# Fifteen small loads behind a copy on ScalarE, in a gated mix of cached attention and a mixer MLP

## The chip, the cores and the metric

The kernel runs on one core of one Trainium2 chip. The metric is the device time of one execution in microseconds (us). The trace is that of one profiled execution; its times count from the start of its span.

## The reference

The inputs are a token `x` for each of two batches (1024 wide), a key and a value cache of 32768 positions (4 key/value heads, 32 query heads, head width 128), and the weights of an attention block A and of a mixer block B. All is fp32. Cut to what matters:

```python
g = sigmoid((x * gate_w).sum(-1))
q = (x @ wq)                                   # 32 heads of 128
a = softmax(q k^T / sqrt(128)) v @ wo          # 8 query heads share a key head
h2 = gelu(layernorm(x1) @ w3) @ w4             # the mixer's MLP
out = g * a + (1 - g) * (x1 + h2)
```

With one position for each batch the mixer's shifts leave zeros, so `x1` is `x`, and `w1` and `w2` are not needed. The caches are by far the most bytes: 8 pairs of batch and head, each with 16 MB of keys and 16 MB of values.

## The kernel before

**The ring.** SBUF holds two large buffers, `load0` and `load1`, 64 KB on each of 128 partitions. All that is read passes through them in halves, two rows of 32 KB side by side for each partition: `wq` (2 halves), `w3` (2), then for each of the 8 pairs the keys `kt` (2 halves) and the values `vt` (2), with `w4` between the fourth and the fifth pair, and `wo` at the end (its last part into a buffer `tail`). A half of a cache or of `wq` is one load of 8 MB; a half of `w3` has 7 MB.

**Who issues.** SyncE (SP) issues all of these loads, in a fixed order, on its own queue, which the profile calls q1. Each load waits on a semaphore that says that its buffer has been read: the half of `kt` for pair 0 waits for TensorE's projection with the `w3` half that lay there; the half of `vt` waits for the scores made from the `kt` half. So at most two loads are in flight or waiting to be read. Two other transfers exist: ScalarE's load of `xg` (the token and the gate's weights, 128 rows of 96 bytes) at the start, on ScalarE's queue, which the profile calls q10, and the store of the output at the end (8 rows of 1 KB), on q1.

**The prologue.** TensorE multiplies `x` by the two halves of `wq` (function `project`, L361, into `sc0` and `sc1`). VectorE copies `sc0` and ScalarE `sc1` to SBUF (L402 and L404, `d_q` and `a_q`). VectorE reorders them (L410), TensorE transposes them (L416), VectorE spreads them into `q_pad` (L424). Then TensorE multiplies the normalised `x` by the halves of `w3`, VectorE copies `sc2` and ScalarE `sc3` (L438 and L440, `d_h` and `a_h`), VectorE reorders (L445, it waits for both), TensorE transposes (L453), VectorE and ScalarE make the gelu (L457 to L472; the Tanh, L462, on ScalarE).

**The turns.** For each pair, `turn` (L479) multiplies the queries by the two halves of `kt` (L488), finds the maximum, lets ScalarE make the exponentials (L555), transposes them (L505), and multiplies them by the two halves of `vt` (L514). On TensorE turn 0 stands behind the prologue's last transposes in program order.

**Waiting.** Each engine runs its instructions in order. `Line.after` puts a wait in front of the engine's next instruction, once for each semaphore value; `Line.mark` raises the engine's own semaphore by one. A load raises its semaphore by 16 when it has landed entirely.

Of the kernel before, what the change touches and what calls it, by code (L numbers as in the profile page):

```python
# [73 lines left out]
def kernel(  # L74
# [52 lines left out]
    nc = tc.nc  # L127
    scale = DH ** -0.5

    def new(name, *shape, parts=P):  # L130
        return nc.alloc_sbuf_tensor(name, [parts, *shape], F32).ap()

    def bank(name):
        return nc.alloc_psum_tensor(name, [P, 512], F32).ap()
# [45 lines left out]
    f = new("f", REP)  # L180
    so_far = new("so_far", D // G)
    out_sb = new("out_sb", 2, CHUNK)

    sc = [bank(f"sc{i}") for i in range(NI)]
    tr = [bank(f"tr{i}") for i in range(2)]
# [9 lines left out]
    def sem(name):  # L195
        cleared.append(nc.alloc_semaphore(name))
        return cleared[-1]

    stored = nc.alloc_semaphore("stored")
    pe, dve, act, pool = (Line(e, sem(n)) for e, n in (  # L200
        (nc.tensor, "pe"), (nc.vector, "dve"), (nc.scalar, "act"), (nc.gpsimd, "pool")))
# [2 lines left out]
    landed = [sem(f"landed{i}") for i in range(2)]  # L204
    w_in = [*landed, sem("w_in2")]
    got_x = sem("got_x")
    issued = sem("issued")
    copied = sem("copied")
    middle = slice(BASE, BASE + 2 * ROWS)
# [192 lines left out]
    d_q = dve.mark(nc.vector.tensor_copy(row[:, 0], sc[0]))  # L402
    act.after(done)
    a_q = act.mark(nc.scalar.copy(row[:, 1], sc[1]))  # L404

    twice = p.rearrange("p i t w q -> p (i t w q)")[:, :REP * P * 2].rearrange(
        "p (h w i q) -> p h w i q", h=REP, w=PART, i=2)
# [33 lines left out]
    n = KF // G  # L441
# [234 lines left out]
```

## Time and profile before

| what | value |
|---|---|
| time, median of 2 runs | 773.13 us (773.12 to 773.14) |
| profiled execution, its own time | 773.23 us |
| its span in the trace | 771.7 us |
| TensorE busy | 437.3 us (57%) |
| VectorE busy | 94.1 us (12%) |
| ScalarE busy | 60.6 us (8%) |
| bytes read | 331.36 MB, mean 429 GB/s over the span |

The profile's page gives the busy time of each engine, the span in 40 slices with the share of time in which the 16 DMA engines were busy, and the DMA queues. The timeline lists instructions as start, duration, engine, line, operation, and in brackets how long the engine had been idle and what ended it. An answer on a window lists the DMA packets that began in it for each queue: number, MB, and their time as a share of 16 engines over the window.

### The profile page before, as it was taken

What the parts mean: (1) busy time and instruction counts of PE and PEld (TensorE: products, weight loads), DVE (VectorE), ACT (ScalarE), POOL (GpSimd) and SP (SyncE); (2) the same over time, 40 slices, a digit from 0 to 9 for tenths busy, and PEclk for the clock granted to TensorE, in tenths of its full rate; (3) what the DMA queues carried; (4) which work ended last, traced back from release to release, by engine and by line L of the source; (5) the groups of instructions that cost most, each with busy time, mean ns of one, the idle gap of its engine ahead of it and who ended that gap; (6) DMA issues with size and microseconds to landing.
All of it is one profiled execution on the core that took longest, in us unless ns stands there. A gap on an engine that the chain in (4) does not pass through costs nothing. (4 is left out here: it accounts for less than half of the span.)

```text
span 771.7 us, 7439 instructions
## 1 busy us (share of the span) xinstructions
PE 437.3 (57%) x3332; PEld 201.3 (26%) x3332; DVE 94.1 (12%) x269; ACT 60.6 (8%) x144; POOL 3.9 (1%) x13
## 2 busy tenths in 40 slices
PE   0576756564645474556575446454745565646467
PEld 0232413231322232223233213121322222313134
DVE  1110202100210021002100002100210021002110
ACT  0000002000200020002000002000200020002000
POOL 2000000000000000000000000000000000000000
PEclk9977668767787768767766678777777687678788
DMA  9999999999999999999999999999999999999997
GB/s 381 435 436 436 435 436 435 432 436 431 435 431 431 435 435 431 435 435 435 427 431 440 432 435 435 435 435 435 435 435 435 435 435 435 435 428 435 425 428 323
DMA packets 6648, 331.50 MB, mean 430 GB/s; under 512 B 872, under 2 KB 1008, under 8 KB 1264
## 3 DMA queue, kind: packets, MB, share of 16 engines
q1 hardware_dynamic: 6496, 331.36, 99.4%
q8 instruction: 7, 0.11, 0.1%
q10 hardware_dynamic: 144, 0.01, 0.0%
q14 instruction: 1, 0.01, 0.0%
HBM read 331.36 MB, written 0.01 MB: 429 GB/s over the span
## 5 line engine op out<-in xcount | busy, mean ns | idle before, releaser
L488 PE MATMUL sc<-load,q_cur 128*32 128x512 f32 x1024 | 145.7, 728 | 131.0 <-PEq L53 131.0
L514 PE MATMUL pv<-load,pt 128*32 128x512 f32 x1024 | 134.4, 684 | 89.4 <-PEq L53 89.4
L488 PEld LDWEIGHTS sc<-load,q_cur 128*32 128x32 f32 x1024 | 52.5, 131 | 218.0 <-issue 212.7
L514 PEld LDWEIGHTS pv<-load,pt 128*32 128x32 f32 x1024 | 40.0, 124 | 173.7 <-issue 173.7
L505 PE MATMUL sc<-wide,p 128*128 128x128 f32 x256 | 43.8, 344 | 22.8 <-PEq L53 22.8
L571 DVE TENSOR_REDUCE mx<-sc 128x1 f32<-128x512 f32 x32 | 21.4, 689 | 285.0 <-PE sc L488 285.0
L555 ACT ACT_TABLE_LOAD x8 | 10.3, 1283 | 484.0 <-ACTq L53 484.0
L505 PEld LDWEIGHTS sc<-wide,p 128*128 128x128 f32 x256 | 39.6, 182 | 30.0 <-issue 30.0
L371 PE MATMUL acc<-load,w_pad 128*32 128x256 f32 x448 | 34.5, 481 | 18.6 <-PEq L53 18.6
L588 DVE COPY pt<-sc 64x256 f32<-64x256 f32 x64 | 25.9, 414 | 80.3 <-PE sc L505 79.7
L561 ACT COPY pt<-sc 64x256 f32<-64x256 f32 x64 | 23.5, 367 | 84.3 <-PE sc L505 81.8
L593 DVE COPY pv_sb<-pv 128x512 f32<-128x512 f32 x16 | 10.3, 686 | 146.8 <-PE tr L520 146.8
L371 PEld LDWEIGHTS acc<-load,w_pad 128*32 128x32 f32 x448 | 18.9, 138 | 33.4 <-issue 28.5
L524 PE MATMUL tr<-sel,pv_sb 128*128 128x8 f32 x128 | 18.7, 282 | 11.8 <-PEq L53 11.8
L357 PE MATMUL sc<-load,x_pad 128*32 128x512 f32 x128 | 18.9, 756 | 6.8 <-PEq L53 6.8
L555 ACT ACTIVATE p<-sc,bias 128x512 f32<-128x512 f32 x32 | 21.5, 685 | 0.1
L524 PEld LDWEIGHTS tr<-sel,pv_sb 128*128 128x128 f32 x128 | 18.2, 226 | 12.3 <-issue 12.3
L357 PE MATMUL sc<-load,xn_pad 128*32 128x384 f32 (+1 forms) x128 | 15.7, 651 | 7.7 <-PEq L53 7.7
L342 PE MATMUL tr<-xg_sb,perm 128*128 128x16 f32 x4 | 1.0, 372 | 23.0 <-DMA xg_sb<-xg 23.0
L584 DVE COPY p<-p 128x256 f32<-128x256 f32 x32 | 9.4, 294 | 26.7 <-ACT p L555 26.7
L357 PEld LDWEIGHTS sc<-load,x_pad 128*32 128x32 f32 x128 | 4.9, 135 | 20.0 <-issue 20.0
L357 PEld LDWEIGHTS sc<-load,xn_pad 128*32 128x32 f32 x128 | 4.8, 131 | 18.5 <-issue 18.5
(89 smaller groups left out, 94.8 us busy)
## 6 DMA issues: line engine op xcount, KB each, us to landing
load<-w SPq DMA_DIRECT2D x4, 7168.0 KB, 24.9
load<-wo SPq DMA_DIRECT2D x1, 7168.0 KB, 29.0
load<-wo SPq DMA_DIRECT2D x1, 4608.0 KB, 19.2
load<-wo SPq DMA_DIRECT2D x1, 2560.0 KB, 24.9
tail<-wo SPq DMA_DIRECT2D x1, 1024.0 KB, 26.9
tail<-wo SPq DMA_DIRECT2D x1, 640.0 KB, 28.0
load<-kt SPq DMA_DIRECT2D x16, 29.8
load<-vt SPq DMA_DIRECT2D x16, 29.4
```

Source lines behind the costliest of these rows:

```text
L357: last = nc.tensor.matmul(b[C * g:C * g + C, :hi - lo], pad[:, k], t[:, o + lo:o + hi], start=(k == 0), stop=(k == KD - 1))
L371: inst = nc.tensor.matmul(acc[C * g:C * g + C], lhsT, rows[:, g * (D // G):(g + 1) * (D // G)], start=False, stop=last, skip_group_check=True)
L488: last = nc.tensor.matmul(sc[i][C * g:C * g + C], q_cur[:, w, s], ring[j][:, w, o:o + 512], start=(s == 0 and w == 0), stop=(s == 1 and w ...
L505: last = nc.tensor.transpose(sc[k][:, t * P:(t + 1) * P], pair.rearrange("p w q -> p (w q)"), ident)
L514: last = nc.tensor.matmul(pv[C * g:C * g + C], pt[j][w][:, lo:lo + C], ring[j][:, w, o:o + G * DH], start=(j == 0 and w == 0 and t == 0), ...
L524: last = nc.tensor.matmul(tr[1][:, w * REP:(w + 1) * REP], pv_sb[:, s, w].rearrange("p i q -> p (i q)"), sel[:, s], start=(s == 0), stop=( ...
L555: nc.scalar.activation(p[:, i, :, :PART], sc[i].rearrange("p (t q w) -> p t w q", t=NT, w=PART), AF.Exp, bias=bias, scale=scale, accum_out ...
L561: nc.scalar.copy(*halves(1, j, c)).then_inc(pt_in, 1)
L571: last = [nc.vector.reduce_max(out=mx[:, k:k + 1], in_=sc[k], axis=AX.X) for k in ((1, 2) if i == 2 else (i,))][-1]
L584: nc.vector.tensor_copy(p[:, i, :, PART], p[:, i, :, 0]).then_inc(to_pe, 1)
L588: nc.vector.tensor_copy(*halves(0, j, c)).then_inc(pt_in, 1)
L593: last = nc.vector.tensor_copy(pv_sb[:, :, :, i], pv.rearrange("p (s q w) -> p s w q", q=HALF, w=PART))
```

## The change

Behind its copy `a_q` of the product with `wq`, ScalarE waits for that copy and issues fifteen loads. Load n (1 to 15) takes the first 16 + n numbers of the first n rows of the keys of pair 0, half 0, from DRAM into a buffer of its own, `told_sb`, on n partitions. Nothing reads that buffer. All fifteen raise a new semaphore, `told`, and ScalarE waits until it stands at 15 x 16, so until all have landed, before its next instruction, the copy `a_h`. Nothing else is changed.

```diff
@@ buffers
     out_sb = new("out_sb", 2, CHUNK)
+    told_sb = new("told_sb", 15, 32, parts=16)
@@ semaphores
     got_x = sem("got_x")
+    told = sem("told")
@@ the prologue
     act.after(done)
     a_q = act.mark(nc.scalar.copy(row[:, 1], sc[1]))
+    act.after(a_q)
+    for n in range(1, 16):
+        nc.scalar.dma_start(told_sb[:n, n - 1, :16 + n], kt[0, 0, :n, :16 + n]).then_inc(told, 16)
+    act.after((told, 15 * 16))
 
```

## The prediction

> **What bounds the kernel now.** I read the page first (the span, the row of DMA shares in 40 slices, the queues), then the timeline of the first 136 us, then the DMA answers for short windows, down to nanoseconds. From the page:
>
> ```profile
> span 771.7 us, 7439 instructions
> ...
> DMA  9999999999999999999999999999999999999997
> ...
> DMA packets 6648, 331.50 MB, mean 430 GB/s; under 512 B 872, under 2 KB 1008, under 8 KB 1264
> ...
> q1 hardware_dynamic: 6496, 331.36, 99.4%
> ...
> q10 hardware_dynamic: 144, 0.01, 0.0%
> ```
>
> The reader is to see a kernel that is one stream of loads: q1 (SP's loads) keeps the 16 DMA engines busy in every slice. q10 is ScalarE's queue; its 144 packets are the one load of `xg`. An instruction anywhere costs time only if it lets q1 run dry or slows its packets; every microsecond in which q1 is dry is a microsecond of the total, since no later slice has room to win it back.
>
> The timeline around the place of the change, as start, duration, engine, line:
>
> ```profile
> 0.73 0.39 ACTq L245 DMA_DIRECT2D xg_sb<-xg  x1
> 0.73 0.88 SPq L246 DMA_DIRECT2D load<-wq  x2
> ...
> 51.97 0.58 ACT L404 COPY pt<-sc 128x512 f32<-128x512 f32 x1 [23.81 <-PE sc L357]
> ...
> 69.76 16.32 SPq L219 DMA_DIRECT2D load<-kt  x2
> ...
> 85.76 0.48 ACT L440 COPY pt<-sc 128x384 f32<-128x384 f32 x1 [33.21 <-PE sc L357]
> ...
> 86.49 2.08 DVE L445 COPY p<-pt 128x896 f32<-128x896 f32 x2
> ...
> 88.62 6.14 PE L453 MATMUL tr<-wide,p 128*128 128x8 f32 x28 [2.92 <-DVE p L445]
> ...
> 96.70 9.76 PE L488 MATMUL sc<-load,q_cur 128*32 128x512 f32 x64 [1.93 <-PEq L53]
> ...
> 106.52 18.60 SPq L219 DMA_DIRECT2D load<-vt  x2
> ...
> 116.05 8.63 PE L488 MATMUL sc<-load,q_cur 128*32 128x512 f32 x64 [9.59 <-PEq L53]
> ...
> 135.40 8.77 PE L514 MATMUL pv<-load,pt 128*32 128x512 f32 x64 [2.03 <-PEq L53]
> ```
>
> SP may load the first half of `vt` at 106.52 only because TensorE has ended the first half of turn 0 (96.70 + 9.76 = 106.46). The halves of `kt` before it have landed by 96.70 and 116.05, where TensorE stood waiting for them: 19.35 us for a load. So the issue at 106.52 comes 9.5 us before q1 would be empty. That is the slack of the stage in which the new wait lies, and it hangs on ScalarE: the copy at 85.76 (L440), VectorE's copies, TensorE's transposes, then turn 0.
>
> **How q10 is served beside q1.** The only load on ScalarE's queue tells it. Below: its landing, the two queues in the first 21.7 us, and four successive records at 21.756, 21.764, 21.772 and 21.776 us.
>
> ```profile
> xg_sb<-xg ACTq DMA_DIRECT2D x1, 12.0 KB, 22.1
> ...
> q1 hardware_dynamic: 128, 8.39, 92.3%
> q10 hardware_dynamic: 112, 0.01, 0.4%
> ...
> q10 hardware_dynamic: 1, 0.00, 18.8%
> ...
> q1 hardware_dynamic: 1, 0.00, 14.1%
> ...
> q10 hardware_dynamic: 1, 0.00, 14.1%
> ...
> q1 hardware_dynamic: 1, 0.07, 3778.1%
> ```
>
> 12 KB took 22.1 us to land. `xg` has 128 rows and 144 packets: 128 of data and 16 that raise the semaphore, 8 + 1 on each engine. By 21.7 us each engine had begun 128/16 = 8 packets of q1 and 112/16 = 7 of q10: one for one. The four records are one engine's: data of q10, semaphore of q1, semaphore of q10, the next 64 KB of q1. So an engine takes one packet from each queue in turn, semaphore packets too; a small packet itself takes some 10 ns (18.8% of 16 engines over 4 ns is 12 ns), but its turn comes only when a q1 packet is through, 19.35/8 = 2.4 us.
>
> The Trainium skill has a rule that speaks against any cost here. Its page "DMA: Bandwidth & Descriptors", section "Queues, rings and completion order", says that an engine drains a whole packet, typically 9 to 17 descriptors, from one queue before it switches. The nine of `xg` would then have gone in one turn, and the trace shows nine turns; by that rule 30 of them would be through in two to four turns (an estimate: some 10 us after the issue), and the sum below would be zero.
>
> **The change, part by part.** Removed or moved: nothing.
>
> *The issues.* ScalarE issues 15 loads from 52.6 (51.97 + 0.58). At 0.39 us each, the row of `xg`, that is 5.9 us, to 58.5; SP's rows bound one by 0.88/2 = 0.44. ScalarE idled 33.21 us there, so this is free under the present order. The bytes: 12.6 KB, nothing against 331 MB.
>
> *How many packets the busiest engine gets.* The nearest row is the store of 8 rows at the end, the one transfer with fewer than 16 rows (window from 771 us):
>
> ```profile
> DMA packets 16, 0.01 MB, mean 12 GB/s; under 512 B 8, under 2 KB 16, under 8 KB 16
> ```
>
> 8 packets of 1 KB and 8 small ones: one engine for each row, each with a semaphore packet. So loads of 1 to 15 rows make 120 + 120 packets. No row says which engines. Spread evenly, an engine gets 15 (perhaps 16); if every load begins at the same engine, that one takes part in all 15 and gets 30. I take 30: nothing in the store or the 46 other transfers shows a memory from one to the next. The low end, 15, is a rival below.
>
> The skill's page named above, section "Why a DMA increments its semaphore by 16 and not by 1", says that SP's and ScalarE's transfers use the lowest-numbered engines, as many as the largest divisor that fits. The 8 + 8 packets agree on the number; which engines, no run here shows yet. By it the figure is 30.
>
> *When the thirtieth is through.* The first is in the ring at about 53.7: q1's first 15 packets begin in the window 1.7 to 2.4 for an issue at 0.73, so 1.0 us behind the start of the issue. From there q1's packets, as begun in 53.7 to 113.5, in 113.5 to 114.0, and in 115.0 to 115.5:
>
> ```profile
> q1 hardware_dynamic: 15, 0.98, 420.3%
> ...
> q1 hardware_dynamic: 464, 25.95, 100.3%
> ...
> q1 hardware_dynamic: 20, 0.66, 303.7%
> ...
> q1 hardware_dynamic: 6, 0.20, 91.2%
> ```
>
> 464/16 = 29 turns by 113.5, the thirtieth with the burst at 113.5 to 114.0 (a few engines trail to 115.5). There `kt`'s second half ends, q1 is empty on that engine, and whatever is left of q10 runs at once: 113.8 is also close to a ceiling. `xg`'s notice came within 0.5 us (last packets before 22.5, landed 0.73 + 22.1 = 22.83). ScalarE's copy L440 therefore starts at 114.4 instead of 85.76, 28.6 us late.
>
> *What stands behind the wait.* On ScalarE the copy L440, the Tanh and the exponentials. VectorE's L445 waits for the copy, TensorE's transposes L453 for VectorE, turn 0 stands behind the transposes on TensorE, and SP's first `vt` behind turn 0. The projections themselves and both `kt` loads do not wait for ScalarE and keep their times.
>
> *The sum.* Copy 0.48, VectorE 2.08, transposes 6.14, some 0.2 between them: 8.9, so turn 0 starts at 123.3. Its first half takes 9.76 (8.63 in the later row, the other bound): 133.1. SP issues, first packets 1.0 later: 134.1. Then 8 packets of 2.4, and 1.0 for spread and notice: the first `vt` half lands at 154.5 instead of 135.3. **The loss is 19.2 us**; counted on an engine that ran dry at 113.8 it is 20.3. I take 19.5. After that the stage has its old slack (the second half of `kt` lies ready, TensorE goes straight through it, the second `vt` issue comes near 141, before 154), and the rest of the program is shifted whole. The profiled execution took 773.23 around its span of 771.7, the median is 773.13: **forecast 792.6**, 2.5% slower. A measurement of this kernel tells about 2% from no change, 788.6.
>
> Where the cover ends: q1 stays fed as long as the copy starts by 113.8 - 1.0 - 9.8 - 8.9 - 0.1 = 94.0. Twenty packets on the busiest engine are free; from there each costs 2.4 us, but for the one that follows a semaphore packet of q1; 28 make about 2%.
>
> **Rivals.**
>
> *The engines share the loads evenly* (not slower). 15 or 16 packets. The second half of `w3` has landed where TensorE starts on it:
>
> ```profile
> 77.35 8.35 PE L357 MATMUL sc<-load,xn_pad 128*32 128x512 f32 x64 [7.66 <-PEq L53]
> ```
>
> Of the 30 turns 9 + 8 come after that (`kt`'s first half with its semaphore, the second's data), so 12 or 13 lie before, and the sixteenth comes 3 packets of 2.4 us later, by 84.5, ahead of 85.76. Time 773.2 to 774. For it: no row shows which engines. Against: it needs a cursor of which no row shows a trace. It decides from 20 packets down. Chance 0.11.
>
> *Several packets go in one turn*, if only a load's data with its semaphore: at most 15 turns, landed by 82, 773.2. The four records speak against it, since q1's packet came between q10's two. Chance 0.03. It is what the Trainium skill's packet rule, named above, would do here.
>
> *The semaphore packets hold their engine up.* If each of the 15 waited for the 64 KB ahead of it to be written, without overlap, the busiest engine would lose up to 2.4 us x 15, and `kt`'s second half would land that much later; even a third of it gives 792.6 + 12 = 804. Against: between q1's and q10's semaphores and the next 64 KB lie 20 ns in the records. Chance 0.05.
>
> *The loads cost less than nothing*: the dry stretch rests TensorE and the clock rises. The stream, not the clock, sets the end. Chance of 2% faster 0.01.
>
> **How the numbers follow.** The forecast's case has 0.80 and reaches from 785 to 797: two or three turns fewer than 30 (27 gives 785), a trailing engine (+1.5), the first half of turn 0 at 8.63 (-1.1), and small packets that each cost 0.1 us instead of 0.01 (+2.5). That is also the range; outside lie the two cases of no cost (0.14), the held engine (0.05) and the rest (0.01). Slower by over 2%: 0.80 less the part below 788.6 (0.06), and 0.05: 0.79. Within 2%: 0.14 and 0.06: 0.20. Faster: 0.01.
>
> **What would show it.** Right: q10 with 144 + 240 = 384 packets; the wait ahead of L440 some 62 us, with that copy at 114 to 116; a hole of near 20 us in q1 from 114 on, seen as two weak slices in the DMA row (the sixth and seventh); every later load late by the same amount. Wrong: the copy still at 85.76 (an even spread, or several packets to a turn); the last small load landing clearly before 105 or after 118; the two `kt` loads landing later than 96.7 and 116 (engine held up); or the hole shrinking in later turns.

## The result, and the profile after

The changed kernel takes 793.58 us (793.5 to 793.65, 2 runs) against 773.13: a ratio of 1.0264, 95% interval 1.022 to 1.0309, slower by 20.45 us. The forecast was 792.6.

The page of the changed kernel:

```profile
span 792.1 us, 7455 instructions
...
DMA  9999972999999999999999999999999999999997
GB/s 421 427 415 431 427 318 107 441 454 421 427 430 424 460 430 424 427 430 424 463 404 453 429 424 453 430 427 430 430 430 453 424 427 437 424 457 427 421 425 336
...
q10 hardware_dynamic: 384, 0.03, 0.0%
```

The span grew by 20.4 us for less than 0.03 MB more on q10. The rows of shares show where it lies: two slices, the sixth and the seventh, in which the stream fell to 318 and 107 GB/s (436 and 435 in the kernel before). In every other slice the DMA engines are as busy as they were. 384 packets are the 144 of `xg` and 240 new ones.

The timeline of the changed kernel around the place (lines have moved by two up to the change, by six behind it):

```profile
51.46 5.53 ACTq L409 DMA_DIRECT2D told_sb<-kt  x15
...
86.52 0.69 DVE L444 COPY pt<-sc 128x512 f32<-128x512 f32 x1 [27.76 <-PE sc L359]
114.82 0.48 ACT L446 COPY pt<-sc 128x384 f32<-128x384 f32 x1 [63.39 <-DMA told_sb<-kt]
115.40 2.08 DVE L451 COPY p<-pt 128x896 f32<-128x896 f32 x2 [28.20 <-ACT pt L446]
117.54 6.14 PE L459 MATMUL tr<-wide,p 128*128 128x8 f32 x28 [31.09 <-DVE p L451]
123.61 15.76 PE L494 MATMUL sc<-load,q_cur 128*32 128x512 f32 x128
...
132.57 7.25 SPq L221 DMA_DIRECT2D load<-vt  x2
...
155.35 4.95 PE L520 MATMUL pv<-load,pt 128*32 128x512 f32 x32 [7.17 <-PEq L53]
```

Read the brackets: ScalarE waited 63.39 us for the small loads, VectorE 28.20 us for ScalarE, TensorE 31.09 us for VectorE. TensorE then goes through both halves of `kt` in one go (128 matmuls in a piece, where before there were two of 64 with a wait between): both had landed. SP's `vt` is issued at 132.57 instead of 106.52. Between 116 and 133.5 us the one packet in the trace is an instruction fetch (q8):

```profile
DMA packets 1, 0.02 MB, mean 1 GB/s; under 512 B 0, under 2 KB 0, under 8 KB 0
...
q8 instruction: 1, 0.02, 0.5%
```

SP's issues from there to the end are late by about the same amount, which is what a lost stretch of the stream looks like. Three of them in the kernel before, and the same three in the changed kernel:

```profile
144.22 20.79 SPq L219 DMA_DIRECT2D load<-kt  x2
...
718.49 21.58 SPq L219 DMA_DIRECT2D load<-wo  x3
...
770.36 0.37 SPq L640 DMA_DIRECT2D out<-out_sb  x1
```

```profile
163.79 20.39 SPq L221 DMA_DIRECT2D load<-kt  x2
...
739.04 22.09 SPq L221 DMA_DIRECT2D load<-wo  x3
...
790.77 0.37 SPq L646 DMA_DIRECT2D out<-out_sb  x1
```

The three are late by 19.57, 20.55 and 20.41 us; the issues between them by 18.4 to 22.0, with no drift.

**The staircase.** Four windows of the changed kernel, each as long as one packet of q1 on every engine, at 55.9 to 57.8, 78.9 to 81.4, 100 to 102.4 and 107.6 to 109.9 us. A line is packets begun, MB, share:

```profile
q1 hardware_dynamic: 16, 0.92, 111.8%
q10 hardware_dynamic: 4, 0.00, 0.2%
...
q1 hardware_dynamic: 16, 1.05, 97.2%
q10 hardware_dynamic: 9, 0.00, 0.3%
...
q1 hardware_dynamic: 16, 1.05, 100.8%
q10 hardware_dynamic: 4, 0.00, 0.1%
...
q1 hardware_dynamic: 16, 1.05, 105.2%
q10 hardware_dynamic: 2, 0.00, 0.1%
```

In each window the 16 engines begin 16 packets of q1 and fewer of q10, in line with one for one. In the first window only four engines had taken up the new packets; later the number fits that of the engines that still have some: 9, 4, 2. If engine e of 0 to 14 takes part in the loads of more than e rows, it has 2 x (15 - e) packets; in the thirteenth or fourteenth turn engines 0 to 8 are left (9), in the twenty-third or twenty-fourth 0 to 3 (4), in the twenty-seventh 0 and 1 (2). That is the uneven deal that the forecast had taken as likelier than the even one.

### The profile page after: what moved, and what is told of

The parts are those of the page before. It is cut to its first block, busy times and chain, and to the rows that moved or that the text cites. A ratio compares the mean times of both kernels' runs of the same rounds, so it can differ in the third digit from the quotient of the medians.

```text
span 792.1 us, 7455 instructions
## 1 busy us (share of the span) xinstructions
PE 434.5 (55%) x3332; PEld 196.7 (25%) x3332; DVE 94.1 (12%) x269; ACT 60.6 (8%) x144; POOL 4.0 (0%) x13
## 3 DMA queue, kind: packets, MB, share of 16 engines
q1 hardware_dynamic: 6496, 331.36, 96.9%
## 5 line engine op out<-in xcount | busy, mean ns | idle before, releaser
L520 PE MATMUL pv<-load,pt 128*32 128x512 f32 x1024 | 134.5, 685 | 93.8 <-PEq L53 93.8
L373 PE MATMUL acc<-load,w_pad 128*32 128x256 f32 x448 | 32.2, 455 | 20.7 <-PEq L53 20.7
L459 PE MATMUL tr<-wide,p 128*128 128x8 f32 x28 | 6.1, 362 | 31.1 <-DVE p L451 31.1
L359 PE MATMUL sc<-load,xn_pad 128*32 128x384 f32 (+1 forms) x128 | 17.8, 728 | 9.3 <-PEq L53 9.3
L459 PEld LDWEIGHTS tr<-wide,p 128*128 128x128 f32 x28 | 6.0, 332 | 31.8 <-DVE p L451 31.8
```

The lines of the kernel that those rows point to most:

```text
L359: last = nc.tensor.matmul(b[C * g:C * g + C, :hi - lo], pad[:, k], t[:, o + lo:o + hi], start=(k == 0), stop=(k == KD - 1))
L373: inst = nc.tensor.matmul(acc[C * g:C * g + C], lhsT, rows[:, g * (D // G):(g + 1) * (D // G)], start=False, stop=last, skip_group_check=True)
L459: last = nc.tensor.matmul(ht_ps[:, o:o + PAIRS], both[:, c, w].rearrange("p i q -> p (i q)"), compact, start=True, stop=True)
L520: last = nc.tensor.matmul(pv[C * g:C * g + C], pt[j][w][:, lo:lo + C], ring[j][:, w, o:o + G * DH], start=(j == 0 and w == 0 and t == 0), ...
```

## The experiments

The theory, "turns": an engine takes one packet from each queue in turn, so a small load lands after as many turns as the busiest engine has small packets, each as long as a packet of q1; and this costs time only where a wait for it lets q1 run dry. Rivals: the small packets slow the stream by themselves; their number in all counts, or the number of loads, or only the semaphores; the engines share them evenly. Each kernel below is the changed kernel with the edit shown, but for half_alone, which is the kernel before with its edit; ratios are against the kernel before, with 95% intervals. The busiest engine's packets are worked out from rows and semaphores, and the runs are there to test that.

| kernel | q10 packets added, all / busiest engine | copy after the wait, us | time, us | ratio |
|---|---|---|---|---|
| rows32 | 48 / 3 | 86.50 | 773.14 | 1.0000 (0.9991 to 1.0009) |
| even240 | 240 / 15 | 86.95 | 773.20 | 1.0001 (0.9991 to 1.0011) |
| one_row_10 | 20 / 20 | 95.12 | 774.89 | 1.0024 (1.0014 to 1.0034) |
| one_row_12 | 24 / 24 | 102.28 | 781.60 | 1.0105 (1.0088 to 1.0122) |
| one_row_15 | 30 / 30 | 114.69 | 793.84 | 1.0270 (1.0253 to 1.0287) |
| rows29 | 30 / 30 | 114.79 | 793.75 | 1.0271 (1.0253 to 1.0288) |
| one_row_20 | 40 / 40 | 115.46 | 794.54 | 1.0274 (1.0257 to 1.0291) |
| rows16x15 | 480 / 30 | 116.49 | 795.26 | 1.0291 (1.0276 to 1.0307) |

**wait_behind: the loads without the harm.**

```diff
-    act.after((told, 15 * 16))
...
     a_h = act.mark(nc.scalar.copy(...))
+    act.after((told, 15 * 16))
```

> The fifteen loads stay, ScalarE waits for them one instruction later, behind its copy of w3's product. Theory of turns (a load costs nothing in itself, only the wait for the packets of the busiest engine does, one turn of q1 for each): the copy is back at 86, turn 0 at 97, no hole in q1, the Tanh starts at about 115 and nothing waits for it that matters: 773 to 774. Rival, the small packets slow the stream or hold their engine up by themselves: the loss stays for the most part, 785 to 793.

773.30 us, ratio 1.0002 (0.9992 to 1.0012). Its timeline on ScalarE and SP:

```profile
85.60 0.48 ACT L445 COPY pt<-sc 128x384 f32<-128x384 f32 x1 [33.34 <-PE sc L359]
...
106.28 0.33 SPq L221 DMA_DIRECT2D load<-vt  x1
114.98 0.30 ACT L468 ACTIVATE u<-u 128x112 f32<-128x112 f32 x1 [28.90 <-DMA told_sb<-kt]
```

The loads land as late as with the change (the Tanh starts at 114.98), and `vt` is issued on time. The same 240 packets beside the same stream cost nothing: the rivals by which they slow it are out.

**even240: the same number of packets, spread.**

```diff
-    for n in range(1, 16):
-        nc.scalar.dma_start(told_sb[:n, n - 1, :16 + n], kt[0, 0, :n, :16 + n]).then_inc(told, 16)
+    for i, n in enumerate((128, 80)):
+        nc.scalar.dma_start(told_sb[:n, i, :17 + i], kt[0, 0, :n, :17 + i]).then_inc(told, 16)
...
-    act.after((told, 15 * 16))
+    act.after((told, 2 * 16))
```

> In place of the fifteen loads two, of 128 and of 80 rows: again 240 packets (208 of data, 32 of semaphores), but 15 on every engine; the wait is where it was. Theory of turns: 15 turns, landed by 84, the copy not later than in the kernel before, 773 to 774. Rival, the number of small packets in all is what costs: 793 as with the change. (Fewer loads too, so the rival that each load costs some 4 us by itself would also give 773; one_row_15 and rows29 tell these apart.)

```profile
86.95 0.48 ACT L446 COPY pt<-sc 128x384 f32<-128x384 f32 x1 [35.17 <-DMA told_sb<-kt]
```

773.20 us. The copy did wait for the loads until 86.95, where they were expected by 84 and the copy no later than before (85.76). one_row_10 below shows a late start of the first packets that would account for it. 86.95 is still far inside the slack, which ends at 94. The number in all is not what costs.

**one_row_15 and rows29: the busiest engine alone.**

```diff
+    for n in range(15):                                                              # one_row_15
+        nc.scalar.dma_start(told_sb[:1, n, :17], kt[0, 0, :1, :17]).then_inc(told, 16)
...
+    nc.scalar.dma_start(told_sb[:29, :17], kt[0, 0, :29, :17]).then_inc(told, 16)    # rows29
```

> Fifteen loads of a single row each: 30 packets in all in place of 240, by the theory all on the same engine. Theory of turns with one and the same first engine: 30 turns, the copy at 114 to 116, 793. If successive loads start on different engines: 2 packets on an engine, landed by 65, 773. If the number of packets in all costs: 30/240 of the loss, 776.

> One load of 29 rows in place of the fifteen. 29 has no divisor from 2 to 16; if the rows are dealt out in equal shares, one engine gets all: 29 packets of data and one of the semaphore. Theory of turns: 30 turns as with the change, one load, 793. Rivals: only semaphore packets, or only the count of loads, cost: 773 to 774. If the rows were spread over 15 or 16 engines: 3 turns, 773.

From the timeline of one_row_15, and from that of rows29:

```profile
114.69 0.48 ACT L446 COPY pt<-sc 128x384 f32<-128x384 f32 x1 [61.79 <-DMA told_sb<-kt]
```

```profile
114.79 0.48 ACT L445 COPY pt<-sc 128x384 f32<-128x384 f32 x1 [63.41 <-DMA told_sb<-kt]
```

Both pages have 174 packets on q10, so 30 new ones, an eighth of the change's, and both kernels take the change's time within 0.3 us. So fifteen loads of one row (of 17 numbers) all go to the same engine, and 29 rows all go to one engine. One semaphore packet in rows29 does what fifteen do in one_row_15: packets count, not semaphores or loads.

**rows32: three rows more.** The edit of rows29 with 32 in place of 29.

> One load of 32 rows in place of one of 29: three rows more, but 32 divides over 16 engines, so 2 packets of data and one of the semaphore on each. Theory of turns: three turns, landed by 63, 773.0 to 773.6, against 793.75 with 29 rows. If what costs is a load with this wait as such, or rows beyond 16: 793.

```profile
86.50 0.48 ACT L445 COPY pt<-sc 128x384 f32<-128x384 f32 x1 [35.07 <-PE sc L359]
```

ScalarE waited for TensorE, not for the load. 773.14 us with 32 rows, 793.75 with 29. The Trainium skill's page "DMA: Bandwidth & Descriptors", section "Why a DMA increments its semaphore by 16 and not by 1", says that such a load uses as many engines as the largest number up to 16 that divides its rows, the lowest-numbered ones; the two kernels agree (1 engine and 16), and the staircase agrees with a fixed first engine.

**one_row_10, one_row_12, one_row_20: the slope and the ceiling.** The edit of one_row_15 with 10, 12 and 20 loads.

> Ten loads of one row: 20 packets on one engine. Theory of turns: the twentieth turn is at about 92, the copy at 93, just inside the slack (break-even 94 to 95): 773 to 775. A loss in proportion to the packets would give 773 + 20 x 20/30 = 787.

> Twelve loads of one row: 24 packets. Theory of turns: the twenty-fourth turn is at 99.3, the copy at 100, 5 to 6 us past the break-even: 778 to 780. In proportion: 789. No slope (a jump somewhere between 10 and 15): 773 or 793.

> Twenty loads of one row: 40 packets. Theory of turns with a ceiling: q1 runs dry at 114 because turn 0 waits, and the packets left over then go one behind the other in well under a microsecond: the copy at 114 to 116.5, 793 to 795, hardly more than with 30. If each packet cost its 2.4 us without a ceiling: the copy near 139, 817.

one_row_10 is at the edge: 1.8 us lost, inside its 773 to 775, with the copy at 95.12 where 93 was expected. one_row_12 misses its 778 to 780 by 1.6 us: its copy starts at 102.28 where 100 was expected, about one turn of 2.4 us. The packets of q1 and q10 in one_row_10 at 52 to 57.9 and 57.9 to 58.3 tell where the time went:

```profile
q1 hardware_dynamic: 38, 2.18, 85.3%
...
q1 hardware_dynamic: 16, 0.46, 265.6%
q10 hardware_dynamic: 2, 0.00, 0.3%
```

The loads were issued from 52.73, and the first of their packets began only after 57.9, over 5 us later; between 52 and 57.9 the engines began 38 packets of q1, 2.4 each on average. The forecast had let the new queue in at the first change of packets behind 53.7. With 20 loads the ceiling is seen bare, in one_row_20 at 114.0 to 114.2:

```profile
q10 hardware_dynamic: 12, 0.00, 3.9%
q1 hardware_dynamic: 3, 0.00, 0.8%
```

The three packets of q1 add up to 0.00 MB: on this engine q1 has run dry, and the 12 small packets still left go in under 0.2 us. Ten packets more than one_row_15 cost 0.7 us, not 24.

**rows16x15: all engines busiest.**

```diff
-        nc.scalar.dma_start(told_sb[:n, n - 1, :16 + n], kt[0, 0, :n, :16 + n]).then_inc(told, 16)
+        nc.scalar.dma_start(told_sb[:16, n - 1, :16 + n], kt[0, 0, :16, :16 + n]).then_inc(told, 16)
```

> Fifteen loads of 16 rows each, so 30 packets on every engine, 480 in all, with the wait where the change has it. Theory of turns (the busiest engine's count alone decides): 30 turns, the slowest engine trails by 1 to 2 us, the copy at 115 to 117, 793 to 796. If the unequal load of the engines were what costs: 773. If the packets in all cost: 480/240 of the loss, 814.

795.26 us, the copy at 116.49. 480 packets, 30 on each engine, cost what 30 on a single one cost in rows29, plus 1.5 us. The last small packets begin between 115.8 and 115.9, where those of the changed kernel begin between 114.0 and 114.2: now the slowest of 16 engines counts.

**half_packets and half_alone: a turn is the other queue's packet.** SP's loads into the two large buffers are made as two each, so that a packet of q1 is half a row. half_alone has the same halving in the kernel before, without the small loads and the wait. The edit, with the first loads of `wq` and the other waits left out:

```diff
-        nc.sync.dma_start(dst, src).then_inc(sem, 16)
+        n = dst.shape[-1]
+        cuts = ((0, n // 2), (n // 2, n)) if sem in landed else ((0, n),)
+        for lo, hi in cuts:
+            nc.sync.dma_start(dst[:, lo:hi], src[:, lo:hi]).then_inc(sem, 16)
...
-            pe.take(landed[T], 16)
+            pe.take(landed[T], 32)
```

> The change as it is, but SP makes each load of the ring as two, each of half a row for every partition: q1's packets are 32 KB (28 KB for w3) in place of 64 KB. Theory of turns: a turn is as long as the other queue's packet, 1.2 us; the thirtieth turn comes at about 82 in place of 114, the copy stays at 86, 773 to 776. Rivals (a fixed price for each load, packet or semaphore): the loss stays, 793.

> The kernel before (no small loads, no wait) with SP's loads each made as two of half the row, as in half_packets. It tells what the 3.2 us are that half_packets still lost, with its copy on time. If they come from the halving itself (twice as many packets, with twice the semaphores, on a stream that sets the end): 776 to 776.5 here too. If they come from the small loads or the wait: 773 to 773.5.

From the timeline of half_packets:

```profile
53.05 5.54 ACTq L413 DMA_DIRECT2D told_sb<-kt  x15
...
86.37 0.48 ACT L450 COPY pt<-sc 128x384 f32<-128x384 f32 x1 [33.35 <-PE sc L363]
```

The same fifteen loads, the same wait, and the copy waits for TensorE again: the loads had landed. It was close: the last small packet begins between 85.4 and 85.5, where the expectation had 82. half_packets takes 776.33 us (ratio 1.0040, 1.0026 to 1.0054), just above its 773 to 776, and half_alone 776.37 (1.0042, 1.0028 to 1.0056). So with turns of half the length the change costs nothing, and the 3.2 us are the halving's own. The load of `xg`, which no edit touched, tells the same with room to spare; in half_alone it lands in 12.6 us, where it took 22.1:

```profile
xg_sb<-xg ACTq DMA_DIRECT2D x1, 12.0 KB, 12.6
```

## Why the prediction was right

*The bound and the place.* Right: the total moved by what q1 lost, between 114 and 133.5, and nothing came back later.

*One for one, and 30 packets on one engine.* Right; even240, one_row_15, rows29 and rows16x15 show that the busiest engine's count decides. The even spread, the rival at 0.11, is refuted by one_row_15. Several packets in a turn is refuted too: ten loads of one row would then have landed by the tenth turn. 20 packets took until 95. The Trainium skill's packet rule (page "DMA: Bandwidth & Descriptors", section "Queues, rings and completion order"), which the prediction weighed, does not hold for these queues: the 30 packets of the one load in rows29 held the copy until 114.79, where the prediction's estimate by the rule was two to four turns.

*The thirtieth turn at 113.8, the copy at 114.4.* The copy came at 114.82. One step towards it was wrong, and the ceiling made up for it. The prediction had the first packet in the ring at 53.7, a delay taken from the start of the kernel, where the queues were empty, and served at the next change of packets. The loads were issued 1.1 us earlier than that working had it (51.46 for 52.6), yet the first of their packets began at 56.0, in one_row_10 over 5 us behind the issue. So every packet came about a turn later, which the ceiling hid at 30 and which shows at 20 and 24 (95.12 for 93, 102.28 for 100). That step was too early by a turn; "twenty packets are free" was too many by about one. That the copy still came within 0.4 us of the forecast is luck: without the ceiling the thirtieth packet would have come one packet of q1 later, near 116.6 (an estimate: 114.2 + 2.4). The low end of the range was mis-sized for the same reason. In one_row_15 one small packet begins between 111.5 and 111.75 and the last three between 113.75 and 114.0, so 27 packets in place of 30 would have saved some 2.4 us (an estimate), and not the 7 of "27 gives 785".

*The chain behind the wait.* 123.3 for turn 0 against 123.61, the issue of `vt` at 133.1 against 132.57 (its first half ran faster than the 9.76 taken). The break-even of 94.0 for the copy holds: the copies at 95.12, 102.28 and 114.82 less the losses by the medians, 1.8, 8.5 and 20.45, give 93.4, 93.8 and 94.4.

*The landing of `vt`.* This term was the one most short. From issue to landing 22.6 us, in the DMA answer for 116 to 133.5:

```profile
load<-vt SPq DMA_DIRECT2D x1, 22.6
```

The sum had 1.0 + 19.4 + 1.0, so 1.2 us less; no run shows what the 1.2 are. With that the loss counted by landings is 155.35 - 135.40 = 19.95 at TensorE, against 19.2 predicted.

*The held engine.* Nothing of it: wait_behind has 15 semaphores on the busiest engine beside a full stream, at 773.30, and TensorE starts on the halves of `kt` at 96.78 and 116.25, against 96.70 and 116.05.

## What to carry to other kernels

Beside a stream of big packets, a small load lands after about (packets on its busiest engine) x (duration of one packet of the other queue), and a few microseconds for the first: 30 packets of at most 124 bytes took 63 us here, until the stream itself ran dry. Give such a load a number of rows that divides over the engines (32 rows landed unnoticed, 29 cost 20.6 us). Make one load where there would be many, since each load adds a semaphore packet on every engine that it uses. Put the wait as late as the program allows; one instruction later made it free. Before pricing a wait by its length, look for when the stream behind it runs dry: the first 43 us of this wait, to 94.4, cost nothing, the rest its full length.

## What the runs showed of the hardware that was not expected

The first packet of ScalarE's queue was slow to start beside the stream: it began 3.4 us behind its issue in half_packets (53.05, first packet between 56.4 and 56.6), 3.5 in one_row_20 (52.56, 56.0), 4.5 in the changed kernel and over 5 in one_row_10. At the start of the kernel, with all queues empty, q1's first packets began 1.0 us behind theirs. A lag of some 3.4 us and then the rest of the packet that is running (up to 2.1 us) fits all four (an estimate). That the lag is not shorter in half_packets, where q1's packets are half as long, speaks against a fixed number of q1's packets going first. What makes the lag is not shown.

Halving the packets of a stream that sets the end from 64 to 32 KB cost 3.2 us of 773. The page of half_alone has 12256 packets on q1 in place of 6496, 360 more on each engine; if they are the whole cost, that is some 9 ns for each (an estimate), about what the records give a semaphore packet (14.1% of 16 engines over 4 ns).
